# Skip term moved from the output products into the last stage of the long convolution

## The chip, the cores and the metric

One core of one Trainium2 chip runs the kernel, in one launch. The metric is the time of one execution on the device, in microseconds (us), as the median of several runs. Beside the runs there is one profiled execution with its trace. Times and windows in the text are us from the start of that execution's span. TensorE executes matrix products, here called products; its trace has a row for products (PE) and one for weight loads (PEld). VectorE is DVE, ScalarE is ACT, GpSimd is POOL, and SyncE (SP) only issues DMAs here; POOL issues some too.

## The reference

Inputs `x`, `k`, `v` are [1, 2048, 1024] in bf16, and the output has the same shape. Cut to what matters:

```
g = sigmoid((x * gate_w).sum(-1, keepdims=True))          # one gate for each time step

# a: a diagonal state space model with 1024 complex states
Lam_bar = exp(dt * Lam);  B_bar = ((Lam_bar - 1) / Lam)[:, None] * Bmat
Bu = einsum("bld,pd->blp", x, B_bar)
h_t = Lam_bar * h_{t-1} + Bu_t                            # over 2048 steps
a = 2 * einsum("blp,dp->bld", h, Cmat).real + x * Dskip   # the second term is the skip term

# b: a short convolution, a product, a long convolution over 2048 steps for each channel
kv = conv4(k, shift_k) * v
b = x * (fft_conv(kv, ssm_k) + kv * ssm_D)

return g * a + (1 - g) * b
```

## The kernel before

**The state space model.** Time is split into 8 phases `ph` (time modulo 8) of 256 steps, the 1024 states into 8 panels `pi` of 128. `load_x(ph)` fetches x of one phase with a DMA transpose into `xT[ph % 4]`, half `ph // 4`. `turnB(pi)` (L780; panels 0 and 1 only) turns the plain loaded B panel `Bn[pi]` over with eight products against the identity matrix for each half, and `evac` (L462, a copy out of PSUM on ACT or DVE) stores it as `BT`. The other panels come by DMA transpose. `gemm(pi, b)` (L828) forms B·x for the phases b and b+4, and `turned` and `fill` run the recurrence (a rotation, a scan on DVE, and products L887 to L934). The states `H` of the first six panels go to DRAM and come back for the output, those of the last two stay. `outp(pt, ph)` (L1035) multiplies the states by C: for one half `pt` of the channels (512 channels; `pt` 0 is channels 512 to 1023), one phase, and two halves `xx` of its steps. One `xx` takes a first part (six panels, 24 products at L1056, 128 rows of weights by 64 columns, 512 wide) and a second part (two panels, 8 such products).

**The skip term** is part of `outp`. For each `outp` a DMA transpose (L1043) fetches the phase of x into a tile `xt`, and eight more products in each first part (L1060, 128 wide) multiply it by `dskd`, a diagonal matrix of Dskip in 128 by 128 blocks that DVE makes once (L489). The result, with g, is taken out of PSUM at once.

**The convolution** runs for 8 groups `u` of 128 channels. `kvprep` makes kv on DVE and ACT. `load_K` loads the filter, with a small addition of ssm_D on POOL (L640). `stage1` (L680: 64 by 64 weights, 32 products in a group) and `spec` (L694: 128 by 64) are two steps of a Fourier transform of length 4096, `product` multiplies the spectra on DVE (L704, L708), `inverse` (L720: 64 rows by 128 columns) and `final` (L733) bring the result back, with a DVE transpose `flip` (L729) in between. `final(u, h)` does four products at L740 (128 by 64 weights, 512 wide) and then multiplies what is in PSUM by x on DVE (L745, `m`). x has been multiplied by 1 - g before (`scale_X`, or `load_Xl` for the channels 512 to 1023).

**The sum.** For channels 0 to 511 (`pt` 1, the last ones to be worked on) DVE reads `outp`'s PSUM, multiplies by g and adds the convolution's part (L1075), and a DMA stores it. For channels 512 to 1023, `outp` leaves g·a in tiles `yt` (L1070, L1072), and `mix(u)` (L1086) adds the convolution's part on DVE and stores it.

**The gates.** `gates` (L944) does 64 products of x with `gate_w` (a tile `gwb`, made from a row of parameters), sends the sums through DRAM, and makes `gcols` (g) and `omgc` (1 - g) from the two exponentials exp(-z) and exp(z) of each step.

**The start.** Rows of parameters (`prow`, `drow` for Dskip, `gwr` for gate_w, `skr` for shift_k) come by DMAs of the ACT queue. PE does 24 warm-up products on the identity (L353), turns three rows of parameters (L357), then `rows` (L477: the rows of Dskip, gate_w and shift_k), then `turnB(0)` (L787), then a second warm-up `keep` (L976, `NWARM` = 32 products), then the first `gemm`. `Bn[1]` is loaded by the SP queue, behind the first two transposes of x.

**What sets the order.** No scheduler runs at build time. Every step is recorded with `op` or `dma`, and three written-out lists decide the rest: `START` has a due time for each of the 1166 steps, and the steps are emitted sorted by it; `OTHER` says which take their second engine (ACT or DVE for a copy, SP or POOL for a DMA); `PLACE` gives each tile its slab and each product group its PSUM banks. Each engine runs its steps in this order and waits on semaphores for what they need.

```
    def planned(self, start, other, place):
        ...
            o.start = st
            if oth:
                o.eng, o.dur, o.fn = o.alt[:3]
        ...
        return sorted(self.ops, key=lambda o: (o.start, o.idx))
```

Of the kernel before, what the change touches and what calls it, by code (L numbers as in the profile page):

```python
# [34 lines left out]
class _Plan:  # L35
# [104 lines left out]
NWARM = 32  # L140
TERMS = (4,4,2,2,2,2,2,2)
START = [
# [122 lines left out]
def kernel(  # L265
# [20 lines left out]
    nc = tc.nc  # L286
# [68 lines left out]
    for s_ in range(2):  # L355
        for h in range(2):
            PE_.matmul(psums[3][64 * h:64 * h + 64, 24 * s_:24 * s_ + 24], lhsT=prow[:, 64 * s_:64 * s_ + 64], rhs=ident[0:24, 0:24],  # L357
                       start=True, stop=True)
# [782 lines left out]
```

## Time and profile before

| | us |
|---|---|
| median of 3 runs | 403.88 (403.58 to 405.85) |
| the profiled execution's own time | 401.83 |
| its span, first to last instruction | 400.0 |
| busy in the span: PE, DVE, ACT, POOL | 379.9, 310.0, 230.9, 47.4 |
| products of PE in the span | 6162 |

The profiled execution is 1.83 us longer than its span, and it is 2.05 us shorter than the median of the runs. Busy PE time is taken up to the modelled end of each product, and products overlap; the distance from the start of one group to the start of the next is the better measure of what a group costs, and the timeline and the chain of work give it.

### The profile page before, as it was taken

The numbers are of one execution on the slowest core, as the hardware profiler recorded it, in microseconds if no ns is written. First come the engines' busy times: TensorE is split into PE (matmuls) and PEld (weight loads), VectorE is DVE, ScalarE is ACT, GpSimd is POOL, SyncE is SP. The second block draws the span as 40 slices with busy tenths as digits, with TensorE's granted clock in tenths as the row PEclk, the third lists the DMA queues.
The fourth block names the chain that finished last, engine by engine and source line by source line (L and its number), as shares of the span: only waits on it lengthen the run. The fifth ranks groups of instructions, "written<-read, shape, count | busy, mean of one in ns | idle before, by whom it ended". The sixth has DMA issues, their size and how long they took to land. (4 is left out here: it accounts for less than half of the span.)

```text
span 400.0 us, 13760 instructions
## 1 busy us (share of the span) xinstructions
PE 379.9 (95%) x6162; PEld 255.4 (64%) x6162; DVE 310.0 (77%) x471; ACT 230.9 (58%) x251; POOL 47.4 (12%) x79
## 2 busy tenths in 40 slices
PE   5899999999999999999999999999999999889990
PEld 4746656665654656576676668667766676676760
DVE  6989878988663787739899878635699776598894
ACT  4799778653655424677498865113633373685550
POOL 1240042022010000003112101120101000000000
PEclk9999999999999999999999999999999999999997
DMA  8999999999764055669999899999679941441334
GB/s 163 184 195 173 171 142 214 207 172 190 152 115 128 28 133 133 157 86 190 261 132 231 186 152 197 180 206 173 100 145 174 202 127 34 156 81 22 62 69 90
DMA packets 153602, 59.12 MB, mean 148 GB/s; under 512 B 135992, under 2 KB 148548, under 8 KB 153544
## 3 DMA queue, kind: packets, MB, share of 16 engines
q1 hardware_dynamic: 149448, 45.64, 66.4%
q0 software_dynamic: 4016, 12.60, 12.9%
q8 instruction: 48, 0.79, 0.9%
q14 instruction: 10, 0.08, 0.1%
q10 hardware_dynamic: 80, 0.02, 0.0%
HBM read 20.48 MB, written 10.49 MB: 77 GB/s over the span
## 5 line engine op out<-in xcount | busy, mean ns | idle before, releaser
L464 ACT CAST slab<-ps 128x1024 bf16<-128x1024 f32 (+1 forms) x188 | 173.2, 972 | 143.5 <-PE ps L680 55.3
L1056 PE MATMUL ps<-slab,slab 128*64 128x512 bf16 x944 | 117.9, 383 | 0.7 <-ACT slab L464 0.5
L464 DVE CAST slab<-ps 128x1024 bf16<-128x1024 f32 (+1 forms) x56 | 61.6, 1113 | 33.9 <-PE ps L680 13.0
L1056 PEld LDWEIGHTS <-slab 128*64 128x64 bf16 x1024 | 68.7, 138 | 29.2 <-issue 1.4
L840 PE MATMUL ps<-slab,slab 128*64 128x512 bf16 (+1 forms) x896 | 83.3, 335 | 0.0
L840 PEld LDWEIGHTS <-slab 128*64 128x64 bf16 x960 | 51.5, 110 | 30.0 <-issue 4.6
L704 DVE TENSOR_TENSOR slab<-slab 128x2048 bf16<-128x2048 bf16 x32 | 39.0, 1219 | 3.8 <-ACT slab L464 3.5
L694 PE MATMUL ps<-slab,Wt 128*64 128x256 bf16 x512 | 34.5, 274 | 0.8 <-DVE slab L745 0.8
L694 PEld LDWEIGHTS <-Wt 128*64 128x64 bf16 x512 | 27.8, 110 | 6.5 <-issue 3.1
L680 PEld LDWEIGHTS <-slab 64*64 64x64 bf16 x2048 | 21.2, 108 | 16.5 <-issue 16.0
L680 PE MATMUL ps<-t,slab 64*64 64x64 bf16 x2048 | 26.6, 195 | 1.3 <-ACT slab L464 1.0
L837 PE MATMUL ps<-slab,slab 128*128 128x512 bf16 (+1 forms) x144 | 25.8, 332 | 1.1 <-ACT slab L464 1.1
L660 DVE TENSOR_TENSOR slab<-slab,slab 128x2047 bf16<-128x2047 bf16 (+2 forms) x20 | 24.3, 1220 | 2.7 <-DMA g_scr<-slab 2.3
L837 PEld LDWEIGHTS <-slab 128*128 128x128 bf16 x176 | 16.8, 98 | 11.9 <-ACT slab L464 1.3
L665 DVE STREAM_TRANSPOSE slab<-slab 128x1024 f32<-128x1024 f32 x8 | 17.0, 2126 | 8.4 <-PE ps L680 4.2
L720 PEld LDWEIGHTS <-Gt 64*128 64x128 bf16 x640 | 18.0, 94 | 7.3 <-issue 6.2
L720 PE MATMUL ps<-slab,Gt 64*128 64x128 bf16 x640 | 22.2, 217 | 0.1
L658 ACT ACTIVATE slab<-slab,skc 128x2045 bf16<-128x2045 bf16 (+2 forms) x10 | 19.9, 2001 | 1.4 <-PE ps L740 0.8
L729 DVE STREAM_TRANSPOSE slab<-slab 128x1024 f32<-128x1024 f32 x16 | 19.2, 1226 | 0.9 <-ACT slab L464 0.7
L708 DVE TENSOR_TENSOR slab<-slab 128x512 bf16<-128x512 bf16 x48 | 18.5, 417 | 0.2
L458 POOL DMA_DIRECT2D slab<-h_scr x12 | 9.1, 761 | 73.1 <-PE ps L1056 27.8
L934 PE MATMUL ps<-slab,slab 128*128 128x512 bf16 x45 | 17.2, 381 | 0.5 <-ACT slab L464 0.5
(192 smaller groups left out, 411.0 us busy)
## 6 DMA issues: line engine op xcount, KB each, us to landing
slab<-h_scr SPq DMA_DIRECT2D x16, 384.0 KB, 4.6
slab<-h_scr POOLq DMA_DIRECT2D x12, 384.0 KB, 5.7
out_dram<-slab SPq DMA_DIRECT2D x32, 128.0 KB, 2.6
slab<-in_B_ssm_k_dram SPq DMA_DIRECT2D x28, 128.0 KB, 4.8
h_scr<-slab POOLq DMA_DIRECT2D x13, 256.0 KB, 4.9
h_scr<-slab SPq DMA_DIRECT2D x11, 256.0 KB, 2.3
slab<-slab POOLq DMA_DIRECT2D x14, 128.0 KB, 4.5
slab<-slab SPq DMA_DIRECT2D x10, 128.0 KB, 5.0
```

The source lines that it names most:

```text
L464: op("ACT", a, lambda: A.copy(o_(), i_()), r=r, w=w, prio=pr, alt=("DVE", d, lambda: V.tensor_copy(o_(), i_())))
L658: alt=("ACT", 2.05, lambda tmp=tmp, j=j, n=n: A.activation(out=tmp.ap[:, 0:n], in_=kT.ap[:, 0:n], func=ACT.Copy, scale=skc[:, u, j:j + 1])))
L660: op("DVE", 1.23, lambda tmp=tmp, j=j, n=n: TT(out=acc.ap[:, j:S], in0=acc.ap[:, j:S], in1=tmp.ap[:, 0:n], op=ALU.add), r=[acc, tmp], w=[a ...
L680: PE_.matmul(ps.ap[64 * r_:64 * r_ + 64, h, i, :], lhsT=av_[64 * h:64 * h + 64, 8 * j + i, :], rhs=t1[64 * h:64 * h + 64, r_].rearrange("p ...
L694: PE_.matmul(ps.ap[64 * e:64 * e + 64, i, r_], lhsT=Wt[:, k2 + e, r_, :], rhs=z.ap[:, k2 + e], start=True, stop=True)
L704: TT(out=T.ap.rearrange("p a b k c -> p a b (k c)"), in0=K.unsqueeze(2).to_broadcast([128, 2, 2, 512]), in1=W_.unsqueeze(1).to_broadcast([ ...
L708: op("DVE", 0.43, lambda i=i, o_=o_: TT(out=T.ap[:, 0, i], in0=T.ap[:, 0, i], in1=T.ap[:, 1, 1 - i], op=o_), r=[T], w=[T], prio=pr)
L720: PE_.matmul(ps.ap[:, h, :, k, :], lhsT=Gt[hs, 4 * q + k].rearrange("p a b -> p (a b)")[:, 64 * (sl + NG - 4):64 * (sl + NG - 2)], rhs=T.a ...
L729: op("DVE", 1.26, lambda: V.transpose(qf.ap.rearrange("p w g e -> p (w g e)").bitcast(F32), qt.ap[:, cs].rearrange("p w k e -> p (w k e)") ...
L837: PE_.matmul(o_, lhsT=BT.ap[:, d, s_].rearrange("p r c -> p (r c)"), rhs=rhs, **kw)
L840: PE_.matmul(o_[64 * ri:64 * ri + 64], lhsT=BT.ap[:, d, ri, s_], rhs=rhs, **kw)
L1056: PE_.matmul(ps.ap[64 * h:64 * h + 64, xx, 0:n], lhsT=H_[:, 2 * h + xx:M:4], rhs=c_.ap[:, k, s_, :], start=(i == 0 and s_ == 0), stop=(i = ...
```

## The change

- The 256 products at L1060, the 16 DMA transposes of `xt`, the matrix `dskd` and the row `drow` are gone.
- The skip term is added in `final`. Since g = (1 - g)·exp(z), x·(1 - g)·(conv + exp(z)·Dskip) has it with the right factor. exp(z) of the steps, as a sum of two bf16 numbers, is turned over by four products (`rt`) after the gates into a tile `Lr`. For each `u` DVE makes a table `Dt` (512 columns) from Dskip and a mask `dmk`. Each `final` does two more products, of weights with 64 rows by 128 columns, 512 wide, into the same PSUM banks. Dskip is loaded into `gwb` by four DMAs of the POOL queue once the gates' products have read it.
- For `u` 5 to 7, ACT takes `final`'s PSUM out and DVE multiplies from SBUF. In `outp` of channels 0 to 511, for phases 0 to 3, ACT multiplies by g and DVE adds from SBUF.
- The start: 16 warm-up products are added behind those of L357, `keep` has 10 products for 32, the row products (5 for 6) come behind the first group of `gemm(0, 0)`, and `Bn[1]` is loaded by the POOL queue.
- `START`, `OTHER` and `PLACE` are new throughout (1175 steps). Slab space grows by 1024 elements for each partition.

```diff
-NWARM = 32
+NWARM = 10
...
-    nc.scalar.dma_start(out=drow, in_=A_Dskip.rearrange("(j p) -> j p", p=128))
...
+    for _ in range(16):
+        PE_.matmul(psums[2][:, 0:128], lhsT=ident, rhs=ident, start=True, stop=True)
...
-    op("DVE", 1.25, lambda: TT(out=dskd, in0=ident.unsqueeze(1).to_broadcast([128, ND, 128]),
-                              in1=dscol.unsqueeze(2).to_broadcast([128, ND, 128]), op=ALU.mult), ...)
...
+        def dtable(k):
+            t = pl.tile("Dt", [512], cap=1)
+            op("DVE", 0.75, lambda: TT(out=t.ap.rearrange("p (a g e) -> p a g e", g=16, e=2),
+                                       in0=gwb[:, k].rearrange("p (w e) -> p w e", e=2).unsqueeze(2).to_broadcast([128, 16, 16, 2]),
+                                       in1=dmk[:, 24:32].bitcast(BF16).unsqueeze(1).unsqueeze(3).to_broadcast([128, 16, 16, 2]), op=ALU.mult),
...
-        def final(qf, u, h, pr):
+        def final(qf, u, h, Dt, pr):
...
-                                   rhs=qf.ap[:, w0:w0 + 16, 16 * t:16 * t + 16, :], start=True, stop=True)
+                                   rhs=qf.ap[:, w0:w0 + 16, 16 * t:16 * t + 16, :], start=True, stop=False)
+                for j in range(2):
+                    PE_.matmul(ps.ap[:, j], lhsT=Lr.ap[64 * j:64 * j + 64, h, :], rhs=Dt.ap[64 * j:64 * j + 64, :],
+                               start=False, stop=True)
...
+            if u >= 5:
+                op("ACT", 1.04, lambda: A.copy(fx(), ps.ap.rearrange("p j w g e -> p g (j w) e")), r=[ps, qf], w=[qf], prio=pr)
+                def mx():
+                    TT(out=xv, in0=fx(), in1=xv, op=ALU.mult)
+                op("DVE", 0.76, mx, r=[qf], w=[(Xl[u], ("q", u, h))], prio=pr)
...
+            op("PE", 0.45, rows, r=[(xT[0], 1)], w=[gps, (e_bn, "rows")], prio=prio("ej"), ni=6)
...
+            dma("POOL", 1.6, lambda: [gwb[64 * j + 32 * v:64 * j + 32 * v + 32] for j in range(2) for v in range(2)],
+                [dv_[j, v].unsqueeze(0).to_broadcast([32, NU, 32]) for j in range(2) for v in range(2)], [], [e_dc], prio("dskd"), issue=0.65)
...
+            def rt():
+                for v in range(2):
+                    for j in range(2):
+                        PE_.matmul(rps.ap[64 * j:64 * j + 64, v, :], lhsT=rx.ap[:, 64 * v:64 * v + 64], rhs=ident, start=True, stop=True)
...
-        op("PE", NWARM * 0.107, keep, w=[wps], prio=-3000, ni=NWARM)
...
-            dma("SP", 1.3, lambda ri=ri: [Bn[1][64 * ri:64 * ri + 64]], [bn_src(1, src)], [], [(e_bl[1], ri)], prio("Bn"))
+            dma("SP", 1.3, lambda ri=ri: [Bn[1][64 * ri:64 * ri + 64]], [bn_src(1, src)], [], [(e_bl[1], ri)], prio("Bn"), alt="POOL")
...
-            dma("SP", 0.2 + 1.1 * n / 512, lambda: [xt.ap], [xf[ph:S:R, ds_]], [], [xt], prio("xt", pt, ph), transpose=True, issue=1.25)
...
-                        for db in range(nu) if i == 0 else ():
-                            for h in range(2):
-                                PE_.matmul(ps.ap[64 * h:64 * h + 64, xx, db * 128:(db + 1) * 128], lhsT=xt.ap[:, db, 2 * h + xx:M:4],
-                                           rhs=dskd[:, u0 + db, :], start=False, stop=False)
...
+                elif ph < 4:
+                    op("ACT", 0.69, lambda xx=xx, g_=g_: A.activation(out=ot.ap[:, xx], in_=ps.ap[:, xx, 0:n], func=ACT.Copy, scale=col(gcols, g_)),
+                       r=[ps, e_gate], w=[(ot, xx)], prio=pr)
+                    op("DVE", 0.44, lambda xx=xx, g_=g_: TT(out=ot.ap[:, xx], in0=ot.ap[:, xx], in1=X[:, g_, ds_], op=ALU.add),
+                       r=done, w=[(ot, xx)], prio=pr)
```

More of the change, by code (lines that the diff above doesn't have):

```diff
@@ L312 @@
     XF = X.rearrange("p g d -> p (g d)")
-    prow, drow, gwr = XF[0:24, 1024:1152], XF[0:8, 1152:1280], XF[0:8, 1280:1408]
+    prow, gwr = XF[0:24, 1024:1152], XF[0:8, 1280:1408]
     skr = XF[0:8, 3072:3072 + 128 * KS]
@@ L434 @@
     Ft = consts.tile([128, 32, 2], BF16, name="Ft")
-    dskd = consts.tile([128, ND, 128], BF16, name="dskd")
-    NSLAB, NPS, CUT = 11, 8, 8
+    dmk = parm.tile([128, 32], F32, name="dmk")
+    NSLAB, NPS, CUT = 11, 8, 6
     slabp = ctx.enter_context(tc.tile_pool(name="slabp", bufs=1))
@@ L467 @@
     e_par, e_cof, e_t1, e_w, e_g, e_ej, e_dskd, e_sk, e_sd = (pl.ext(n) for n in ("par", "cof", "t1", "w", "g", "ej", "dskd", "sk", "sd"))
-    e_h, e_gscr, e_gate, e_x, e_bn = (pl.ext(n) for n in ("hs", "gs", "gate", "x", "bn"))
+    e_dc, e_h, e_gscr, e_gate, e_x, e_bn = (pl.ext(n) for n in ("dc", "hs", "gs", "gate", "x", "bn"))
     op("DVE", 0.1, lambda: None, w=[e_par], prio=-2000)
     dma("POOL", 0.6, lambda: [sdz[0:128:32]], [B_ssm_D.rearrange("(u b c) -> b u c", b=4, c=32)], [], [e_sd], prio("sk"), issue=1.3)
-    dscol = parm.tile([128, 8], F32, name="dscol")
-    gps = pl.psum([2, 512])
-    def rows():
-        PE_.matmul(gps.ap[:, 0, 0:8], lhsT=drow, rhs=ident[0:8, 0:8], start=True, stop=True)
-        PE_.matmul(gps.ap[:, 1, 0:8], lhsT=gwr, rhs=ident[0:8, 0:8], start=True, stop=True)
-        for k in range(KS):
-            PE_.matmul(gps.ap[:, 0, 8 + 8 * k:16 + 8 * k], lhsT=skr[:, k::KS], rhs=ident[0:8, 0:8], start=True, stop=True)
-    op("PE", 0.45, rows, w=[gps], prio=prio("ej"), ni=6)
-    def rows2():
-        V.tensor_copy(dscol, gps.ap[:, 0, 0:8])
-        V.tensor_copy(skc, gps.ap[:, 0, 8:8 + 8 * KS].rearrange("p (k u) -> p u k", k=KS))
-        V.tensor_copy(gwb, gps.ap[:, 1, 0:8].unsqueeze(2).to_broadcast([128, ND, 32]))
-    op("DVE", 0.75, rows2, r=[gps], w=[e_ej, (e_sk, 1)], prio=prio("ej"))
-    op("DVE", 1.25, lambda: TT(out=dskd, in0=ident.unsqueeze(1).to_broadcast([128, ND, 128]),
-                              in1=dscol.unsqueeze(2).to_broadcast([128, ND, 128]), op=ALU.mult), r=[e_ej], w=[e_dskd], prio=prio("dskd"))
     def coefs():
@@ L590 @@
     tables0()
+    Lr = pl.tile("Lr", [2, 128], cap=1)
     xT = [pl.tile("xT", [ND, 2, M], cap=4) for _ in range(4)]
@@ L731, in flip @@
                r=[qt], w=[qf], prio=pr)
-        def final(qf, u, h, pr):
+        def dtable(k):
[3 more added lines that the diff above has]
+                                       in1=dmk[:, 24:32].bitcast(BF16).unsqueeze(1).unsqueeze(3).to_broadcast([128, 16, 16, 2]), op=ALU.mult),
+               r=[e_dskd, e_dc], w=[t], prio=prio("dt", k))
+            return t
+        def final(qf, u, h, Dt, pr):
             ps = pl.psum([2, 16, 16, 2])
@@ L740, in f @@
                         PE_.matmul(ps.ap[64 * t:64 * t + 64, j], lhsT=Ft.rearrange("p a b -> p (a b)"),
-                                   rhs=qf.ap[:, w0:w0 + 16, 16 * t:16 * t + 16, :], start=True, stop=True)
-            op("PE", 2 * MM(512), f, r=[qf, e_t1], w=[ps], prio=pr, ni=4)
+                                   rhs=qf.ap[:, w0:w0 + 16, 16 * t:16 * t + 16, :], start=True, stop=False)
+                for j in range(2):
+                    PE_.matmul(ps.ap[:, j], lhsT=Lr.ap[64 * j:64 * j + 64, h, :], rhs=Dt.ap[64 * j:64 * j + 64, :],
+                               start=False, stop=True)
+            op("PE", 3 * MM(512), f, r=[qf, e_t1, Dt, Lr], w=[ps], prio=pr, ni=6)
             def m():
@@ L745, in m @@
                 TT(out=xv, in0=ps.ap.rearrange("p j w g e -> p g (j w) e"), in1=xv, op=ALU.mult)
+            if u >= 5:
+                fx = lambda: qf.ap.rearrange("p w g e -> p (w g e)")[:, 0:1024].rearrange("p (g w e) -> p g w e", g=16, e=2)
+                op("ACT", 1.04, lambda: A.copy(fx(), ps.ap.rearrange("p j w g e -> p g (j w) e")), r=[ps, qf], w=[qf], prio=pr)
+                def mx():
+                    xv = x_view(u)[:, :, 64 * h:64 * h + 64].rearrange("p g (w e) -> p g w e", e=2)
+                    TT(out=xv, in0=fx(), in1=xv, op=ALU.mult)
+                op("DVE", 0.76, mx, r=[qf], w=[(Xl[u], ("q", u, h))], prio=pr)
+                return
             op("DVE", 1.23, m, r=[ps] + ([] if u in Xl else [(e_x, ("s", k)) for k in range(4)]), w=[(Xl.get(u, e_x), ("q", u, h))], prio=pr)
@@ L766, in conv @@
                 inverse(pp, TERMS[u], qt, q, pr + 3.0)
+            Dt = dtable(u)
             for h in range(2):
@@ L769, in conv, with param_rows, rows, rows2 @@
                 flip(qt, qf, h, prio("fl", u, h))
-                final(qf, u, h, prio("fl", u, h) + 1.0)
+                final(qf, u, h, Dt, prio("fl", u, h) + 1.0)
     def s5():
+        def param_rows():
+            gps = pl.psum([2, 512])
+            def rows():
+                PE_.matmul(gps.ap[:, 1, 0:8], lhsT=gwr, rhs=ident[0:8, 0:8], start=True, stop=True)
+                for k in range(KS):
+                    PE_.matmul(gps.ap[:, 0, 8 + 8 * k:16 + 8 * k], lhsT=skr[:, k::KS], rhs=ident[0:8, 0:8], start=True, stop=True)
+            op("PE", 0.45, rows, r=[(xT[0], 1)], w=[gps, (e_bn, "rows")], prio=prio("ej"), ni=6)
+            def rows2():
+                V.tensor_copy(skc, gps.ap[:, 0, 8:8 + 8 * KS].rearrange("p (k u) -> p u k", k=KS))
+                V.tensor_copy(gwb, gps.ap[:, 1, 0:8].unsqueeze(2).to_broadcast([128, ND, 32]))
+            op("DVE", 0.75, rows2, r=[gps], w=[e_ej, (e_sk, 1)], prio=prio("ej"))
+            def dmask():
+                TS(out=dmk[:, 0:1], in0=wi, scalar1=15.5, scalar2=-16.0, op0=ALU.is_gt, op1=ALU.mult)
+                TT(out=dmk[:, 0:1], in0=dmk[:, 0:1], in1=wi, op=ALU.add)
+                TS(out=dmk[:, 1:17], in0=iota_row[:, 0:16], scalar1=dmk[:, 0:1], scalar2=None, op0=ALU.is_equal)
+                V.tensor_copy(dmk[:, 24:32].bitcast(BF16), dmk[:, 1:17])
+            op("DVE", 0.65, dmask, r=[e_par], w=[e_dskd], prio=prio("dskd"))
         def loadB(pi):
@@ L952, in f @@
                                        start=(d == 0 and e == 0), stop=(d == ND - 1 and e == 1))
-            op("PE", 1.95, f, r=list(xT) + [e_ej], w=[ps], prio=prio("ga"), ni=64)
+            op("PE", 1.95, f, r=list(xT) + [e_ej], w=[ps, e_dc], prio=prio("ga"), ni=64)
+            dv_ = A_Dskip.rearrange("(u v j c) -> j v u c", v=2, j=2, c=32)
+            dma("POOL", 1.6, lambda: [gwb[64 * j + 32 * v:64 * j + 32 * v + 32] for j in range(2) for v in range(2)],
+                [dv_[j, v].unsqueeze(0).to_broadcast([32, NU, 32]) for j in range(2) for v in range(2)], [], [e_dc], prio("dskd"), issue=0.65)
             row = pl.tile("grow", [2, M], F32, cap=1)
@@ L968, in dv @@
             def dv():
+                TS(out=zg[:, 2, :], in0=zg[:, 2, :], scalar1=1.0e26, scalar2=None, op0=ALU.min)
+                V.memset(rx.ap, 0.0)
+                V.tensor_copy(rx.ap[:, 0:16], zg[:, 2, :])
+                TT(out=rx.ap[:, 16:32], in0=zg[:, 2, :], in1=rx.ap[:, 0:16], op=ALU.subtract)
+                V.tensor_copy(rx.ap[:, 96:128], rx.ap[:, 0:32])
                 TS(out=zg[:, 1:3, :], in0=zg[:, 1:3, :], scalar1=1.0, scalar2=None, op0=ALU.add)
@@ L971, in dv @@
                 V.reciprocal(omgc, zg[:, 2, :])
-            op("DVE", 0.6, dv, r=[e_z], w=[e_gate], prio=prio("gb"))
+            rx = pl.tile("rx", [128], cap=1)
+            op("DVE", 1.0, dv, r=[e_z], w=[e_gate, rx], prio=prio("gb"))
+            rps = pl.psum([2, 128])
+            def rt():
+                for v in range(2):
+                    for j in range(2):
+                        PE_.matmul(rps.ap[64 * j:64 * j + 64, v, :], lhsT=rx.ap[:, 64 * v:64 * v + 64], rhs=ident, start=True, stop=True)
+            op("PE", 4 * MM(128), rt, r=[rx], w=[rps], prio=prio("gb"), also=[Lr], ni=4)
+            evac(lambda: Lr.ap, lambda: rps.ap, r=[rps], w=[Lr], pr=prio("gb"), half=True)
         wps = pl.psum([512])
@@ L982, in s5 @@
         for ri, src in enumerate((A_B_re, A_B_im)):
-            dma("SP", 1.3, lambda ri=ri: [Bn[1][64 * ri:64 * ri + 64]], [bn_src(1, src)], [], [(e_bl[1], ri)], prio("Bn"))
-        BTs = [turnB(0), turnB(1)]
+            dma("SP", 1.3, lambda ri=ri: [Bn[1][64 * ri:64 * ri + 64]], [bn_src(1, src)], [], [(e_bl[1], ri)], prio("Bn"), alt="POOL")
+        BTs = [turnB(0)]
+        op("PE", NWARM * 0.107, keep, r=[(e_bn, (0, 1))], w=[wps], prio=-3000, ni=NWARM)
+        BTs.append(turnB(1))
         for ph in (0, 4, 1, 5, 2, 6, 3, 7):
             load_x(ph)
-        for k in range(4):
-            load_X(k)
         Hs = {}
@@ L997, in s5 @@
                 gemm(pi, b, BTs[pi], mt_, H)
+                if pi == 0 and b == 0:
+                    param_rows()
+                    for k in range(4):
+                        load_X(k)
             if pi == 0:
@@ L1041, in outp @@
             ds_ = slice(128 * u0, 128 * u0 + n)
-            xt = pl.tile("xt", [nu, M], cap=2, hold=True)
-            dma("SP", 0.2 + 1.1 * n / 512, lambda: [xt.ap], [xf[ph:S:R, ds_]], [], [xt], prio("xt", pt, ph), transpose=True, issue=1.25)
             ot = None if late else pl.tile("ot", [2, n], cap=4)
@@ L1057, in f @@
                                            start=(i == 0 and s_ == 0), stop=(i == NP - 1 and s_ == 1))
-                        for db in range(nu) if i == 0 else ():
-                            for h in range(2):
-                                PE_.matmul(ps.ap[64 * h:64 * h + 64, xx, db * 128:(db + 1) * 128], lhsT=xt.ap[:, db, 2 * h + xx:M:4],
-                                           rhs=dskd[:, u0 + db, :], start=False, stop=False)
-                op("PE", 2 * ni * MM(n) * 1.02 + nu * 0.057, lambda f=f: f(0, ni), r=[xt, e_dskd, Ht] + [CT[i, pt][0] for i in range(0, ni, 2)] + done,
-                   w=[(ps, xx)], prio=pr, also=[yt[xx] if late else ot], ni=4 * ni + 2 * nu)
+                op("PE", 2 * ni * MM(n) * 1.02, lambda f=f: f(0, ni), r=[Ht] + [CT[i, pt][0] for i in range(0, ni, 2)] + done,
+                   w=[(ps, xx)], prio=pr, also=[yt[xx] if late else ot], ni=4 * ni)
                 op("PE", 2 * (NP - ni) * MM(n) * 1.02, lambda f=f: f(ni, NP), r=[Hs[i][ph % 4] for i in range(ni, NP)] + [CT[i, pt][0] for i in range(ni, NP, 2)],
```

218 rows, old and new, of tables (OTHER, PLACE, START) are left out of this document.

## The prediction

> **What bounds the kernel now.** The page comes first: PE is busy nearly all of the span.
>
> ```profile
> PE 379.9 (95%) x6162; PEld 255.4 (64%) x6162; DVE 310.0 (77%) x471; ACT 230.9 (58%) x251; POOL 47.4 (12%) x79
> ```
>
> The windows (engine, busy us, instructions) say where PE is not. It loses 6 us before 20, 2.4 us in 340 to 360, and some tenths in a few other stretches. From 60 to 380 the windows' rows lack 5.0 us in all.
>
> ```profile
> 0.00:20.00 20.00, 13.95 (x135) 12.46 (x136) 15.56 (x82) 12.08 (x17) 4.06 (x14) 1.00 0.96 173
> 180.00:200.00 20.00, 19.20 (x398) 13.10 (x394) 18.47 (x20) 12.09 (x14) 5.55 (x9) 1.00 1.14 225
> 200.00:220.00 20.00, 19.28 (x368) 13.40 (x364) 19.26 (x29) 18.20 (x19) 3.87 (x6) 1.00 1.14 182
> 340.00:360.00 20.00, 17.64 (x428) 13.15 (x428) 15.67 (x20) 15.23 (x16) 0.00 (x0) 1.00 0.44 119
> 360.00:380.00 20.00, 19.49 (x412) 14.24 (x410) 17.30 (x23) 11.13 (x12) 0.00 (x0) 1.00 0.22 42
> ```
>
> The chain of waits ends on PE until 389.7 and then on DVE. It also prices groups of products from start to start.
>
> ```profile
> 384.40 1.00 PE ps L720 x32
> 385.40 1.44 PE ps L1056 x12
> 386.84 0.23 PE ps L1060 x8
> 387.08 2.16 PE ps L1056 x20
> 389.24 0.45 PE ps L740 x4
> 389.69 0.02 issue
> 389.71 1.22 DVE slab L745
> 390.93 1.32 DVE slab L1075 x2
> 392.25 1.14 DVE slab L745
> ```
>
> So a kernel with less work on PE is shorter by that work, if PE's waits, the start and the tail stay. I go through these four.
>
> **PE's work.** The skip products cost 0.23 us for eight (L1060), at 32 places: -7.5 us. In their place each of the 16 `final` groups gets two products, 512 wide. Twenty such at L1056 take 2.16 us, 0.108 each, because two run side by side in halves of the columns. The new ones lie in halves of the rows. The nearest row is L720, also 64 rows by 128 columns: two groups, 32 products of 128 columns, in 1.00 us, 31 ns each with what is added below, where a quarter of 0.108 is 27. So row halves overlap too, and I take 0.216 for two: +3.5 us. Without overlap it would be +6.9; under 3.5 it cannot be, since both are 512 wide.
>
> A change of the weights' shape has its own price. The timeline shows it:
>
> ```profile
> 345.92 0.60 PE L740 MATMUL ps<-slab,Ft 128*64 128x512 bf16 x4
> 346.45 0.62 PE L720 MATMUL ps<-slab,Gt 64*128 64x128 bf16 x16
> 389.07 0.60 PE L740 MATMUL ps<-slab,Ft 128*64 128x512 bf16 x4
> 389.50 1.03 PE L1056 MATMUL ps<-slab,slab 128*64 128x512 bf16 x8
> ```
>
> The four products of `final` take 0.43 us when the next group has their shape, and 0.53 when it is 64 by 128: 0.10 for a change. The new `final` changes shape inside (16 times), and in the built order of the changed kernel neighbouring groups differ at 210 places from panel 1 on, against 195. That is 31 changes: +3.1 us. The count is exact; at 0.09 to 0.12 for one it is 2.8 to 3.7. [...]
>
> `rt` (four products, 128 wide) and the row products, now in the stream, add 0.4 us. PE's work: -7.5 + 3.5 + 3.1 + 0.4 = **-0.5 us**. The change buys almost nothing there.
>
> **The start.** PE's row products wait for parameter rows, and everything behind them waits too:
>
> ```profile
> PE ps L478 <- DMA X<-in_A_Dskip_dram: 2.3, 1, 2.3
> PE ps L481 <- DMA X<-in_B_shift_k_dram: 1.3, 1, 1.3
> ```
>
> `turnB(0)` starts at 8.46, its copies end at 11.47, `keep` runs to 13.3, four groups of panel 0 to 16.76, and the first product of panel 1 starts at 19.05. In the new order `turnB(0)` waits for `Bn[0]` alone: issued at 1.99, 4.3 us to landing, 6.3. But POOL now issues `Bn[1]` at about 1.8, in front of the load of ssm_D (wanted only at 40 us), and 512 KB more at the 298 GB/s of that stretch take 1.7 us from `Bn[0]` and from x, so 6.3 to 8.0; I take 7.2. Copies then end at 10.2; four groups of 0.87 and the rows give 13.9, or 14.4 if the second half of x (before by about 11) comes 1.7 later. Then `turnB(1)` and three copies on ACT. Before, PE went on after two copies, 2.3 us; in the new order the half it needs first is copied last, 3.3 us. Panel 1 starts at 17.2 to 17.7 for 19.05: **-1.4 us**, lower bound -2.2.
>
> The other bound comes from PE's rate. The 32 products of `keep` take 3.39 us, 106 ns each; sixteen of `turnB(0)` take 1.89 us, of `turnB(1)` 1.06. PE ran at half rate until about 13, 4.6 us into its first unbroken stretch. In the new start 44 products fill 1.4 to about 6.1, then comes a gap. If that does not count, four groups and two `turnB` at half rate cost about 4 us: +2.6. [...]
>
> **The tail.** PE's last `inverse` ends at 385.40. Behind it PE has `outp` work until 391, and DVE is done at 394.7, 3.7 us later. In the new order only two second parts (2 x 0.92) are left behind the last `inverse`, so PE waits for a copy (1.0) and two flips (1.23 each): it gets about 1.1 us later. Behind the last `final` stand an ACT copy (1.02), a multiply (0.68, as L1086) and two sums (1.3): 3.4 us with the hand-overs. **+0.8 us.**
>
> **PE's waits.** In 340 to 360 what ends PE's waits is DVE (L745, L729) and ACT's copies. DVE loses there two `final` reads (1.22 to 0.68) and four L1075 (0.745 to 0.42, as L708): 2.4 us of its 15.7. Of the 2.4 us of waits I take 2.0 to go, and 1.0 of the 2.6 elsewhere, since a new order moves them all: **-3.0 us**, between -5 (all go) and +3 (one more stretch like 340 to 360).
>
> **Costed at nothing.** Eight `Dt` tables on DVE (0.42 to 0.68 each, hidden by a DVE that idles 90 us; uncovered +5). The copies moved to ACT (6 x 1.02 + 8 x 0.69 = 11.6 us, hidden by its idle 42%; see the rivals). The 16 transposes off SP: DMAs are busy in 180 to 320 but end none of PE's waits. A wait is added on POOL: the four loads of Dskip wait for the gates' products (about 39 us), and behind them, four issues of 0.76 us, stands the addition that group 0's filter needs, then `stage1` on PE. Before, it was due as soon as the filter had landed. Other products are queued ahead of it; uncovered it costs 1 to 2 us.
>
> **Sum.** -0.5 - 1.4 + 0.8 - 3.0 = -4.1 us. The profiled execution (span 400.0, 1.8 us around it) would go from 401.83 to 397.7. The median lies 2.05 us above it; from 403.88 I get **399.8 us**.
>
> **Rivals.** A measurement of this kernel can tell 0.5%, 2.0 us, from no change.
> - *The waits stay.* Each removed wait is replaced by another, since the order is new everywhere. For it: the rows of 180 to 220, where DVE is busy 19.3 of 20, are touched by no edit but the added tables. Against it: the lighter DVE after 320. Sum -1.1: 402.8.
> - *ScalarE bounds the end.* All 14 added passes fall between 320 and 390, where ACT is busy 42 of 72 us; it would be 54 of 69, and it serves in order, so copies that free PSUM for PE stand behind passes that wait for a whole `outp`. In 340 to 360, at about that load on both engines, PE lost 2.36 of 20; over 70 us that is 8.3, against 2.9 now: +5.4. With the waits elsewhere as they are: 403.88 - 1.1 + 5.4 = 408.2, slower. It decides if PE loses over 7 us between 320 and its end, with ACT as the last to release. Against it: DVE gives up as many passes.
> - *The start stays at half rate*: +2.6 for -1.4, 403.8.
> - *Row halves do not overlap*, so the narrow products cost what they replace: 399.8 + 3.5 = 403.3.
>
> **How the numbers follow.** The forecast 0.64, waits stay 0.12, ScalarE 0.17, half rate 0.04, no overlap 0.03. The forecast's own range, with its bounds on start and waits not all at one end, is 394.5 to 403. The range reaches over the three cases near no change to 405.5 and leaves out ScalarE and a few in a hundred below. Faster by over 0.5% (under 401.9): the forecast and a little of the second case, 0.66; within: 0.16; slower: 0.18.
>
> **What would show it.** In the changed profile: the first panel-1 product at 17 to 18; 16 narrow pairs at 0.22, and 0.10 around them; PE's windows after 320 fuller than now; 3.4 us from the last `final` to DVE's end. I am wrong if panel 1 starts after 19, if ACT ends most of PE's late waits, or if stretches without an edit gain or lose over 2 us.

## The result and the profile after

The changed kernel takes 398.99 us (median of 20 runs, 396.94 to 404.58) where the kernel before takes 403.51 (20 runs, 401.08 to 413.46). The ratio is 0.989, 95% interval [0.987, 0.992], so it is faster by 4.4 us; 399.8 was forecast. Ratios here and below leave out executions that were disturbed.

The profiled execution after took 401.38 us (span 399.6), 2.4 above that kernel's median, and the one before 401.83, below its own. The two traces differ by 0.45 us where the medians differ by 4.5. So this trace holds something that most executions don't, and the first question is what. The page and the windows:

```profile
PE 380.4 (95%) x5935; PEld 246.4 (62%) x5935; DVE 306.2 (77%) x481; ACT 243.0 (61%) x271; POOL 45.5 (11%) x78
```

```profile
0.00:20.00 20.00, 14.24 (x127) 11.88 (x128) 14.89 (x81) 12.72 (x18) 3.11 (x12) 1.00 0.97 184
20.00:40.00 20.00, 20.00 (x98) 9.81 (x97) 15.57 (x30) 16.28 (x19) 4.81 (x8) 0.91 1.03 185
240.00:260.00 20.00, 18.55 (x288) 12.94 (x286) 16.26 (x21) 8.06 (x9) 1.80 (x3) 1.00 1.10 179
340.00:360.00 20.00, 19.44 (x368) 12.99 (x366) 16.81 (x23) 13.66 (x16) 0.00 (x0) 1.00 0.29 70
360.00:380.00 20.00, 19.71 (x341) 13.74 (x341) 14.92 (x20) 13.50 (x16) 0.00 (x0) 1.00 0.27 60
```

The late rows are as forecast: PE lacks 0.56 us in 340 to 360, where it lacked 2.36, though ACT has the added copies (27.2 us in the two last rows, 26.4 before). Two rows are new. In 20 to 40 the granted clock (the third figure from the end) is 0.91, and in 240 to 260 PE lacks 1.45 us where it lacked nothing. The row of 240 to 260 before:

```profile
240.00:260.00 20.00, 20.00 (x346) 15.03 (x344) 14.17 (x18) 7.03 (x8) 2.29 (x4) 1.00 1.02 188
```

The list of PE's waits names what is behind them (us in total, times, longest):

```profile
PE ps L812 <- DMA X<-in_A_B_im_dram: 2.3, 1, 2.3
PE ps L664 <- POOL slab L624: 2.3, 2, 1.5
PE ps L862 <- ACT slab L465: 2.0, 1, 2.0
```

L812 is `turnB`, L862 `gemm`, L664 `stage1`; L465 is `evac`, and L624 POOL's addition in `load_K`. The timeline of PE shows the first and the third:

```profile
8.44 1.87 PE L812 MATMUL ps<-ident,X 128*128 128x128 bf16 x16 [2.31 <-DMA X<-in_A_B_im_dram]
11.41 1.89 PE L862 MATMUL ps<-slab,slab 128*128 128x256 bf16 x8
...
16.23 1.06 PE L812 MATMUL ps<-ident,X 128*128 128x128 bf16 x16
19.33 4.88 PE L862 MATMUL ps<-slab,slab 128*128 128x512 bf16 x14 [2.04 <-ACT slab L465]
```

`turnB(0)` starts at 8.44, no earlier than before (8.46), though the parameter rows no longer stand in front of it: `Bn[0]` itself lands only at 8.3. `Bn[1]` is being loaded beside it. The first group of `gemm(0, 0)` takes 1.89, where it takes 1.03 at the full clock (in `a_k4`, one of the experiments). Then PE waits 2.04 us for three copies in a row on ACT, and panel 1 starts at 19.33 (before: 19.05). The trace's clock records give full rate from 13.76, half rate from 20.59 to 24.00, and full rate again.

The end of the kernel, PE's timeline and then the chain of waits:

```profile
389.05 0.62 PE L732 MATMUL ps<-slab,Ft 128*64 128x512 bf16 x4 [0.53 <-DVE slab L713]
389.61 0.39 PE L735 MATMUL ps<-slab,slab 64*128 64x512 bf16 x2
390.18 0.62 PE L732 MATMUL ps<-slab,Ft 128*64 128x512 bf16 x4 [0.18 <-DVE slab L713]
390.74 0.39 PE L735 MATMUL ps<-slab,slab 64*128 64x512 bf16 x2
```

```profile
391.17 1.02 ACT slab L743
392.19 0.02 issue
392.21 0.70 DVE slab L747
392.92 0.02 issue
392.94 0.69 DVE slab L1130
```

The narrow pair (L735) starts 0.56 after the wide products and takes 0.39 to its modelled end. PE waits 0.7 us for the two flips, and from its end (391.13) to DVE's end (394.23) it is 3.1 us.

### The profile page after: what moved, and what is told of

It is laid out like the page before. It is cut to its first block, busy times and chain, and to the rows that moved or that the text cites. A ratio compares the mean times of both kernels' runs of the same rounds, so it can differ in the third digit from the quotient of the medians.

```text
span 399.6 us, 13332 instructions
## 1 busy us (share of the span) xinstructions
PE 380.4 (95%) x5935; PEld 246.4 (62%) x5935; DVE 306.2 (77%) x481; ACT 243.0 (61%) x271; POOL 45.5 (11%) x78
## 4 chain that ended last, share of the span: by engine, by line
PE 88%; ACT 4%; DVE 3%; DMA 2%; POOL 1%; issue 1%; SPq 0%; DVEq 0%; POOLq 0%; ACTq 0%
PE ps L1099 27%; PE ps L865 22%; PE ps L862 7%; PE ps L678 6%; PE ps L664 5%; PE ps L704 5%; ACT slab L465 3%; PE ps L959 3%; PE ps L887 2%; PE ps L732 2%; PE ps L940 2%; DMA X<-in_A_B_im_dram 2%; PE ps L942 1%; PE ps L735 1%; DVE slab L688 1%
## 5 line engine op out<-in xcount | busy, mean ns | idle before, releaser
L465 ACT CAST slab<-ps 128x1024 bf16<-128x1024 f32 (+1 forms) x191 | 176.2, 971 | 126.4 <-PE ps L664 30.4
L1099 PE MATMUL ps<-slab,slab 128*64 128x512 bf16 x944 | 112.8, 383 | 0.0
L465 DVE CAST slab<-ps 128x1024 bf16<-128x1024 f32 (+1 forms) x54 | 58.5, 1099 | 39.7 <-PE ps L664 15.8
L862 PE MATMUL ps<-slab,slab 128*128 128x256 bf16 (+1 forms) x176 | 31.7, 340 | 2.1 <-ACT slab L465 2.0
L664 PEld LDWEIGHTS <-slab 64*64 64x64 bf16 x2048 | 21.2, 108 | 19.5 <-issue 15.6
L664 PE MATMUL ps<-t,slab 64*64 64x64 bf16 x2048 | 27.1, 195 | 2.9 <-POOL slab L624 2.3
L644 DVE TENSOR_TENSOR slab<-slab,slab 128x2047 bf16<-128x2047 bf16 (+2 forms) x24 | 29.2, 1218 | 0.3
L862 PEld LDWEIGHTS <-slab 128*128 128x128 bf16 x176 | 17.7, 102 | 14.9 <-ACT slab L465 2.5
L459 POOL DMA_DIRECT2D slab<-h_scr x13 | 9.9, 760 | 84.2 <-PE ps L1099 39.4
L459 POOL DMA_DIRECT2D h_scr<-slab x12 | 6.9, 572 | 95.2 <-DVE slab L465 60.3
```

Source lines behind the costliest of these rows:

```text
L465: op("ACT", a, lambda: A.copy(o_(), i_()), r=r, w=w, prio=pr, alt=("DVE", d, lambda: V.tensor_copy(o_(), i_())))
L644: op("DVE", 1.23, lambda tmp=tmp, j=j, n=n: TT(out=acc.ap[:, j:S], in0=acc.ap[:, j:S], in1=tmp.ap[:, 0:n], op=ALU.add), r=[acc, tmp], w=[a ...
L664: PE_.matmul(ps.ap[64 * r_:64 * r_ + 64, h, i, :], lhsT=av_[64 * h:64 * h + 64, 8 * j + i, :], rhs=t1[64 * h:64 * h + 64, r_].rearrange("p ...
L862: PE_.matmul(o_, lhsT=BT.ap[:, d, s_].rearrange("p r c -> p (r c)"), rhs=rhs, **kw)
L1099: PE_.matmul(ps.ap[64 * h:64 * h + 64, xx, 0:n], lhsT=H_[:, 2 * h + xx:M:4], rhs=c_.ap[:, k, s_, :], start=(i == 0 and s_ == 0), stop=(i = ...
```

## The experiments

All kernels but those named `b_` start from the changed kernel. A due time that is moved is given by the step's number.

**The changed kernel again, and the late sums back on DVE.** `a_same` has no edit. `a_latedve`:

```diff
-op("ACT", 1.04, lambda: A.copy(fx(), ps.ap...), r=[ps, qf], w=[qf], ...)
+op("ACT", 1.04, m, r=[ps, qf], w=[qf], ...)          # m: DVE, out of PSUM
-op("DVE", 0.76, mx, ...)
+op("DVE", 0.76, lambda: None, ...)
...
-op("ACT", 0.69, lambda ...: A.activation(out=ot.ap[:, xx], in_=ps.ap[:, xx, 0:n], func=ACT.Copy, scale=col(gcols, g_)), ...)
+op("ACT", 0.69, lambda ...: STT(out=ot.ap[:, xx], in0=ps.ap[:, xx, 0:n], scalar=col(gcols, g_), in1=X[:, g_, ds_], ...), ...)
-op("DVE", 0.44, lambda ...: TT(out=ot.ap[:, xx], in0=ot.ap[:, xx], in1=X[:, g_, ds_], op=ALU.add), ...)
+op("DVE", 0.44, lambda: None, ...)
```

> The changed kernel as it is, for a second profile and as the base of the other runs: 399.0 us (ratio to before 0.987 to 0.992). The first profile has PE idle for 2.0 us ahead of panel 1 (17.3 to 19.3) and then half the clock from 20.6 to 24.0. If the idle stretch alone brings this, it is there again, and 1.7 us with it. If it also depends on how the clock's own windows fall, it can be missing here with the same idle stretch; the profiled execution is then about 1.7 us nearer to 399.

> The changed kernel with the late sums back on VectorE: for groups 5 to 7 VectorE multiplies out of PSUM as before, and for phases 0 to 3 of the last outputs it multiplies by g and adds in one pass out of PSUM; ScalarE's 14 passes are left out. If the lighter VectorE is where the 2 us of waits after 320 went: +1.5 to +3 us, 400.5 to 402, with PE's row of 340 to 360 back near 17.6 to 18.5 of 20. If ScalarE's passes hold the end up: -1 to -3 us, 396 to 398, with a shorter stretch behind PE's last inverse. If the order alone removed the waits: within 0.7 us of 399.

`a_same`: 399.49 us, ratio 0.989 [0.985, 0.993]; its profiled execution took 398.61. PE's timeline and a window of it:

```profile
12.96 3.92 PE L862 MATMUL ps<-slab,slab 128*128 128x256 bf16 x24
16.72 1.06 PE L812 MATMUL ps<-ident,X 128*128 128x128 bf16 x16
20.04 6.21 PE L862 MATMUL ps<-slab,slab 128*128 128x512 bf16 x28 [2.27 <-ACT slab L465]
```

```profile
240.00:260.00 20.00, 20.00 (x328) 13.96 (x326) 16.60 (x21) 7.38 (x8) 2.45 (x4) 1.00 0.97 181
340.00:360.00 20.00, 19.44 (x386) 13.18 (x388) 15.98 (x25) 15.46 (x17) 0.00 (x0) 1.00 0.36 81
```

PE's wait ahead of panel 1 is there again, 2.27 us, and the half rate behind it is not: the expectation that the idle stretch alone brings it fell. Nor is the wait in 240 to 260 there. Without these two the execution is 2.8 us shorter than the first, although panel 1 started 0.7 later. So both are chances of an execution, not a constant cost. Where the clock's own steps fall, the other branch of the expectation, tells these two apart, but not `a_latedve` (last section).

`a_latedve`: 401.73 us, ratio 0.995 [0.992, 0.998], 0.6% or 2.4 us slower than `a_same`; the two intervals overlap by 0.001. The windows, and PE's waits after 320:

```profile
340.00:360.00 20.00, 18.28 (x346) 12.35 (x346) 17.38 (x25) 12.19 (x13) 0.00 (x0) 1.00 0.36 81
360.00:380.00 20.00, 19.37 (x348) 13.92 (x343) 17.07 (x19) 9.54 (x10) 0.00 (x0) 1.00 0.18 41
```

```profile
PE ps L732 <- DVE slab L713: 1.3, 2, 0.8
PE ps L664 <- DVE slab L1114: 1.3, 1, 1.3
```

PE lacks 2.35 us from 320 to 380, for 0.85 with the sums on ACT and 2.87 in the kernel before. So 1.5 of the 2.0 us gained there come from the late sums, and 0.6 more behind 380, where the last flip waits behind a sum on DVE. ScalarE as the bound of the end is refuted: with its passes taken away the kernel is slower. The load that this rival assumed never came either. From 320 to PE's end ACT is busy 42.0 us in the first profile after, as before, and not 54: with the passes added, the new order gives it 34 plain copies there for 44, and DVE 13 for 8.

**The two kernels without a skip term.** `b_noskip` (and once more `b_noskip2`) is the kernel before without the loop of L1058 to L1061; `a_nonarrow` is the changed kernel without the narrow pair:

```diff
-rhs=qf.ap[:, w0:w0 + 16, 16 * t:16 * t + 16, :], start=True, stop=False)
+rhs=qf.ap[:, w0:w0 + 16, 16 * t:16 * t + 16, :], start=True, stop=True)
-for j in range(2):
-    PE_.matmul(ps.ap[:, j], lhsT=Lr.ap[64 * j:64 * j + 64, h, :], rhs=Dt.ap[64 * j:64 * j + 64, :], start=False, stop=True)
```

> The kernel before without the 256 skip products (the skip term is left out of the output; its transposes and the diagonal matrix stay). By the prediction's price, 32 places of 0.23 us, and PE as the bound: 403.5 - 7.4 = 396.1 us, ratio 0.982. If other engines' waits take the place of a part of it (DVE late, or DMAs in the middle): 398 to 402.

> The kernel before without the 256 skip products once more (the skip term is left out of the output), since the first run of it gave a wide interval (ratio 0.972 to 0.991) and a profile that can't be read. By the prediction's price ratio 0.982 and a span near 393, with outp groups of 2.6 us where skip products stood in them; if the products were partly covered: 0.985 to 0.992.

> The changed kernel without the two narrow products of each final (the skip term is left out of the output; the tables Dt, the turned exponentials and all copies stay). By the prediction's price, 16 x (0.22 for the pair + 0.10 or 0.20 for shape changes): 399.0 - 5.1 to 6.7 = 392.3 to 393.9 us, ratio to before 0.972 to 0.976. If the two kernels without a skip term differ by 2 to 4 us, that difference is what order, start and late copies bring; if they are within 1 us of each other, the change's gain came from cheaper skip products alone. If late waits hide the pair: 396 to 399.

`b_noskip` gave 0.981 [0.972, 0.991], `b_noskip2` 0.983 [0.977, 0.988], 397.2 us: 7.1 us by the second, where 7.4 were priced. The profiled execution of `b_noskip` took 628.95 us and is not used. `a_nonarrow`: 0.976 [0.971, 0.981], 5.1 us less than `a_same`, at the lower end of 5.1 to 6.7. Its profile, one of its long executions (400.69 us), shows what can take the rest. The wait for the late filter has grown to 4.3 us, and the granted clock of that window fell to 0.83 (PE's waits, then the window):

```profile
PE ps L664 <- POOL slab L624: 5.1, 2, 4.3
```

```profile
240.00:260.00 20.00, 15.70 (x228) 9.84 (x223) 14.12 (x18) 6.91 (x8) 1.71 (x3) 0.83 1.01 161
```

The skip work costs 7 and 5 us in the two kernels, which the intervals do not tell apart. The two kernels without it differ by 0.6% (0.9825 and 0.976), 2.5 us, which is the rest of the change: order and late sums. Their intervals overlap, so the size of this is not settled by them alone.

Where the time goes can be added up from the trace. For each product from panel 1 on, the distance to the next product's start, summed by kind (us; a wait counts with the product ahead of it):

| | before | b_noskip2 | after | a_same | a_latedve |
|---|---|---|---|---|---|
| `outp` | 122.63 | 116.55 | 116.17 | 116.18 | 116.15 |
| `final` | 7.24 | 7.24 | 13.67 | 13.67 | 14.33 |
| `rt` | 0 | 0 | 0.21 | 0.21 | 0.21 |
| `gemm` | 125.69 | 125.49 | 128.51 | 126.61 | 126.62 |
| `spec` | 32.31 | 32.30 | 29.85 | 29.85 | 31.05 |
| `stage1` | 26.19 | 27.52 | 25.89 | 24.35 | 24.53 |
| all others | 57.48 | 57.67 | 57.10 | 57.09 | 57.20 |
| sum | 371.54 | 366.77 | 371.40 | 367.96 | 370.09 |

The swap is -6.45 in `outp`, +6.43 in `final` and +0.21 for `rt`: +0.2 us, nothing. The gain of 3.6 us in `a_same` is in `spec` and `stage1` (-4.3), kinds whose products the change does not touch. Of these 4.3 us 3.5 are recorded idle time of PE (4.55 before, 1.08 in `a_same`). But over all kinds the idle time fell only from 5.0 to 3.6 us, since other waits came in; the 0.9 us more in `gemm` are mostly POOL's wait near 48. The other 2.2 us of the gain are products that start closer together: 0.5 in the three kinds of the swap without their waits, and 1.6 spread over the rest, 0.7 of it in `spec`. No run shows the cause of these 1.6; idle time is counted from the modelled end of a product, so short waits can hide in them. In the first profile after, `gemm` is 1.9 us higher (the half rate) and `stage1` 1.5 (the filter of group 4), and the gain on PE is gone.

**The start.** `a_bnsp` loads `Bn[1]` by SP behind the first transpose of x; `a_turn` puts `turnB(1)` ahead of two groups of `gemm(0, 0)` and takes that gemm's copy to DVE.

```diff
 # a_bnsp: the two loads of Bn[1]
-START[22], START[23] = 5.3, 5.95;    OTHER[22] = OTHER[23] = 1    # POOL
+START[22], START[23] = 5.0, 5.03;    OTHER[22] = OTHER[23] = 0    # SP
 # a_turn: turnB(1), and the copy of gemm(0, 0)
-START[31], START[29] = 14.04, 14.493;    START[51], OTHER[51] = 14.17, 0    # ACT
+START[31], START[29] = 11.60, 11.65;     START[51], OTHER[51] = 16.12, 1    # DVE
```

> The changed kernel with the two loads of Bn[1] on the SP queue, behind the first transpose of x, where POOL issued them beside Bn[0]. If they are what holds Bn[0] back: Bn[0] has landed by 6.3 to 6.8 instead of 7.6 to 8.4, turnB(0) starts then, and panel 1 starts 0.8 to 1.5 us earlier than in the other profiles of this kernel (19.1 to 20.8); time -0.5 to -1.5 us against 399.3. If Bn[0] comes at 7.5 to 8.4 all the same, something else sets it (the other loads of the start), and the time stays within 0.5 us. In both cases the clock's rise can move by whole steps of 3.4 us, worth up to 2 us in one execution.

> The changed kernel with turnB(1) moved ahead of the last two groups of gemm(0, 0), and with that gemm's copy on VectorE instead of ScalarE. If the three copies in a row on ScalarE are what PE waits for ahead of panel 1 (2.0 to 2.3 us in four profiles): the wait shrinks to 0.9 to 1.4 us, panel 1 starts 0.9 to 1.3 us earlier, 398.0 to 398.4 us. If VectorE, which gets 1.2 us more there, then holds up something of the recurrence: no gain.

In `a_bnsp` `Bn[0]` is there when the warm-up ends (PE's timeline):

```profile
6.21 1.34 PE L812 MATMUL ps<-ident,X 128*128 128x128 bf16 x16
...
13.89 3.45 PE L862 MATMUL ps<-slab,slab 128*128 128x256 bf16 x16 [2.43 <-DMA slab<-in_A_x_dram]
```

`turnB(0)` starts at 6.21; in eight profiles with `Bn[1]` on POOL it is 7.5 to 8.7. In `a_all` and `a_all2` below, also with `Bn[1]` on SP, it is 6.5 and 6.2. So the loads side by side do hold `Bn[0]` back, by 1.0 us or more. But the second half of x now comes later, PE waits 2.43 us for it, and panel 1 starts at 20.27. The time is 399.59, ratio 0.989 [0.983, 0.995]: no gain is shown. The first theory was right on the load; on the time the runs do not bear it out.

`a_turn`: 398.15 us, 0.983 [0.977, 0.989]. Its PE line:

```profile
18.96 5.34 PE L862 MATMUL ps<-slab,slab 128*128 128x512 bf16 x24 [1.32 <-DVE slab L465]
```

The wait ahead of panel 1 is 1.32 for 2.04 to 2.27. The ratio is 0.6% under `a_same` and the intervals overlap, so a gain is not shown. In its profile, one of its long executions (403.94 us), PE waits 3.5 us for a load of states at 226.7, where nothing was moved, and the granted clock from 220 to 240 is 0.91.

**The late filter.** `a_kpool` issues POOL's addition for group 0 ahead of the Dskip loads and lets POOL load the filter of group 4; `a_k4` puts that load ahead of two loads of states as well.

```diff
 # a_kpool
-START[84] = 40.056;    START[712], OTHER[712] = 229.511, 0    # SP
+START[84] = 42.7;      START[712], OTHER[712] = 227.5, 1      # POOL
 # a_k4: as a_kpool, and
+START[712], START[1024], START[1031] = 225.95, 225.96, 225.97
```

> The changed kernel with POOL's addition for group 0's filter ahead of the four loads of Dskip, and with the load of group 4's filter issued by POOL at about 227 instead of by SP at 237. If these two places are what PE waits for as 'stage1 for POOL's addition' (0.8 to 1.5 us near 48, and 0 to 4.3 near 252, as the load happens to land): both waits are gone from the profile, and the median falls by 1 to 2 us from 399.3 to 397.3 to 398.3. If the next thing is late right behind them (ScalarE's copies of stage1, Dskip's tables): the waits show under another name, and the time stays at 399.

> The changed kernel with group 4's filter loaded by POOL ahead of the two loads of states for phases 3 and 4 (in the run before, POOL stood at these two until 235, so the filter was issued at 236.6, no earlier than by SP in the changed kernel), and group 0's addition ahead of the Dskip loads. The filter should be issued at about 228 and POOL's addition end by 243; PE's stage1 wants it at 249 to 252. If the late filter is a cost of the changed order: no wait of stage1 for POOL's addition near 250, and the median 1 to 2 us under 399.3. If it is rarely late without a profile: no difference.

`a_kpool`: 400.37 us, 0.989 [0.983, 0.996]. The wait near 48 is gone (PE's row of 40 to 60 is 20.00 for 19.19), the other is not. POOL's timeline and PE's wait:

```profile
236.63 3.15 POOL L459 DMA_DIRECT2D slab<-in_B_ssm_k_dram  x4 [0.48 <-issue]
...
254.09 0.33 POOL L624 TENSOR_TENSOR slab<-slab,sdz 128x32 bf16<-128x32 bf16 x1 [9.52 <-DMA slab<-in_B_ssm_k_dram]
```

```profile
PE ps L664 <- POOL slab L624: 4.5, 1, 4.5
```

The first of the load's four parts was issued hardly earlier than by SP (238.64 in the first profile, 237.44 in `a_same`), since POOL stood at loads of states in front of it. All four were issued by 239.8, where SP took until 246.5 in the first profile, and yet POOL's addition could start only at 254.09. In `a_all`, with the same edit, the load was issued at 235.49 and the addition started at 247.71. So the time from issue to landing differs by several us from one execution to the next, and the issue time alone does not set it. In `a_k4` the loads of states stand behind it, and it still went out only at 235.34, with POOL idle for 12.5 us ahead of it and no releaser shown. The memory that the filter goes to is then what holds it; that is argued from the list of places, not shown. POOL's addition now ends at 244.9, and `stage1` no longer waits. But the states' loads come later, and PE waits for them at 246 to 248 in all three profiles with this edit (0.8 us in `a_k4`, 3.3 and 1.6 in `a_turnk4` and `a_all2` below), and in no other profile of the changed kernel at that place:

```profile
PE ps L1099 <- DMA slab<-h_scr: 0.8, 1, 0.8
```

The ratio is 0.990 [0.986, 0.995], no gain. The theory that this one load is the cost fell. From 180 to 240 the DMA engines are busy for 0.86 to 1.10 of the time in all profiles of the changed kernel and its variants, and here the load that went ahead left PE waiting 0.8 to 3.3 us for others.

**Together.** `a_all` has the edits of `a_bnsp`, `a_turn` and `a_kpool`; `a_turnk4` those of `a_turn` and `a_k4`; `a_all2` all of `a_turnk4` and `a_bnsp`.

> The three edits together (Bn[1] on SP, turnB(1) earlier with a copy on VectorE, the two filter edits). If each removes a wait on the path that ends last, they add up: -2.4 to -4.5 us, 395 to 397 us, ratio to before 0.979 to 0.983. If an earlier start only makes PE wait longer at the next late load (as where the narrow products were left out, 4.3 us near 252), the sum is no better than the best of them.

> turnB(1) ahead of the last two groups of gemm(0, 0) with a copy on VectorE, and the early filter of group 4. If both are on the path: 396 to 397.5, ratio to before 0.978 to 0.982. If only the start counts, about 398 (0.983).

> The same with Bn[1] on SP behind the first transpose of x. That brought turnB(0) 1.2 to 2 us earlier, but PE then waited 1.0 to 2.4 us for the second half of x. If the sum counts: 395 to 396.5, ratio 0.975 to 0.980. If x takes the gain back: the same as without this edit.

`a_all`: 0.982 [0.975, 0.990]; `a_turnk4`: 0.993 [0.989, 0.998]; `a_all2`: 0.988 [0.982, 0.995]. The profiled execution of `a_all` is the shortest of all, 395.61 us (span 393.8). Its panel 1 starts at 16.65 (16.45 in `a_all2`), once panel 0 has begun the only loads that PE waits for are those of x (1.0 and 0.9 us, before 25), and the clock is full from 5.40 until PE is done. That of `a_turnk4` has a wait for states in 240 to 260, and a granted clock of 0.83 there:

```profile
PE ps L1099 <- DMA slab<-h_scr: 3.3, 1, 3.3
```

The edits do not add up, and no version is shown to beat the changed kernel: the intervals of the two best hold its 0.989.

## Why the prediction was right, step by step

- **PE's work, -0.5.** Measured +0.2 with the waits that fall in it (the table), -0.5 without them. The pair in halves of the rows overlaps: in the first profile its two products start within 5 ns of each other, and a `final` takes 0.42 us more than before, the price of 0.216 and two changes of shape at 0.10. The rival without overlap is out. What TensorE does in the 0.10 us of a change no run shows.
- **The start, -1.4.** This step failed. Panel 1 started at 18.3 to 20.8 in six profiles with the changed start (19.05 and 19.86 in two with the old one): about 0. Two links were wrong. `Bn[0]` was taken to land at 7.2, and with `Bn[1]` beside it `turnB(0)` can start only at 7.5 to 8.7. The 298 GB/s behind the 7.2 hold for one slice of 0.9 us; the six slices behind it average 226, which makes the 1.7 us 2.3. And the full clock was counted on: in the first profile `turnB(0)` and the first group run at half rate, 0.8 us more each (1.87 and 1.89 for 1.05 and 1.03 in `a_kpool`). The half-rate rival, at 0.04, was too low as a mechanism, though its +2.6 was too high.
- **The tail, +0.8.** Too high by 0.7. PE waits 0.7 us for the flips, not 1.1, and DVE ends 3.1 us behind PE, 0.6 earlier than before. The prediction's own three rows add up to 3.0; the hand-overs that made them 3.4 take some hundredths each in the chain.
- **PE's waits, -3.0.** After 320 they went from 2.87 to 0.85: -2.0, as the prediction has it for that stretch, 1.5 of it by the late sums (`a_latedve`). From 60 to 320 they are 1.1 in `a_same` for 2.1, the other -1.0, but 2.6 in the first profile.
- **POOL's wait** was flagged at 1 to 2 us: 0.8 in both profiles, and `a_kpool` removes it. The late filter of group 4 was not seen, though the order of the queue held a part of it: SP issued its first part at 230.3 before, and at 238.6 after.
- **The sum** held as errors cancelled, and that is luck. The profile of `a_same` is 3.2 us shorter than the one before, for -4.1: the start gives +1.0 (-1.4 taken), PE's work -0.5, the waits -3.0, the tail +0.1 (+0.8 taken), POOL's wait +0.8 (nothing taken), and the products set closer together -1.6, which no term foresaw. The first profile is only 0.45 us shorter. The step from profile to median is luck too: the median was taken to lie 2.05 us above the profile, and it lies 0.9 above that of `a_same` and 2.4 below the first one. One of the prediction's own signs for being wrong came true (panel 1 after 19), and another came near (a stretch without an edit, 240 to 260, lost 1.5 us, short of the 2 set).
- **ScalarE bounds the end** is refuted by `a_latedve`, and its condition, 54 us of ACT's time, did not arise (42.0); **the waits stay** holds for the middle of the kernel in some executions, not for its end.

## What to carry to other kernels

When work moves from many small products to few, price it from start to start, shape changes included: here 256 products gave way to 32 and PE's work stayed nearly the same. About half of the gain, 2.4 of 4.4 us, came from the engine that lost its passes over PSUM late in the kernel; where the rest comes from is not settled. A load moved to another queue and issued beside the load that is wanted first held that one back by 1.0 us or more here, and in a stretch with a DMA share of 0.86 to 1.10 moving one load ahead made PE wait 0.8 to 3.3 us for others; look at the issue time of each load in the new order against the time when its reader wants it, and leave room for landing times that differ by several us (the filter of group 4 was ready 17.5 us after its first issue in `a_kpool`, 12.2 in `a_all`). Take a second profile of the same kernel before a difference of 2 us is explained.

## What the runs showed of the hardware

- **The clock goes by steps.** In the clock records of the profiles before and after, the stretches at one rate within the kernel last 3.41, 6.83, 368.64 and 382.29 us, which is 1, 2, 108 and 112 times 3.413. Six more profiles have windows of 20 us with a granted clock of 0.91 or 0.83, which fits 3.41 or 6.83 us at half rate. Where a step falls differs from one execution to the next: the same start reached the full clock that lasted beyond it at 10.6, 13.4, 13.8, 15.3 and 17.0 us (`a_k4`, `a_latedve`, the first profile, `a_same`, `a_nonarrow`).
- **A long wait cost more than itself.** With waits of 3.3, 3.5, 4.3 and 4.5 us in the middle of the kernel (`a_turnk4`, `a_turn`, `a_nonarrow`, `a_kpool`) the granted clock of the window with the wait was 0.83, 0.91, 0.83 and 0.91. That fits half rate for 6.83 or 3.41 us, so that PE lost about 3.4 or 1.7 us more (half of that time, an estimate). Waits of 2.0 to 2.3 us ahead of panel 1 brought a clock of 0.91 in 20 to 40 in 2 of 7 profiles (the first one and `a_bnsp`, with 2.04 us; `a_kpool` and `a_k4`, also with 2.04 us, kept 1.00).
- **Where a wait falls among the steps tells some cases apart, not all.** Steps of 3.413 us are counted here from those times of the full clock. In the first profile the 2.04 us ahead of panel 1 lie in one step, 17.17 to 20.59, and half rate followed. In `a_same` a step's end at 18.7 cuts the 2.27 us into 0.95 and 1.32, and the full clock stayed. But in `a_latedve` 2.26 of the 2.27 us lie in one step, 16.8 to 20.2, and the full clock stayed too. How much idle time in a step brings half rate these runs do not settle.
